# Where the maxima of a chunk are split and turned in a fused attention and GLU kernel: VectorE alone, or VectorE, GpSimd and VectorE in three successive periods

## The chip, the cores and the metric

The kernel runs on one core of a Trainium2 chip. The metric is the time of one execution on the device in microseconds (us), lower is better. The kernel before takes 1719.04 us (median of three runs, 1718.17 to 1721.21).

## What is computed

The input `x` is 2048 tokens by 512 features, all fp32. Half A is a full softmax attention with 32 heads of 16 features. Half B is a GLU with 1792 hidden features. A gate per token mixes the two.

```python
g = sigmoid((x * gate_w).sum(-1, keepdims=True))
qkv = (x @ wqkv).reshape(B, S, 3, H, Dh).transpose(2, 0, 3, 1, 4)
scores = einsum("bhqd,bhkd->bhqk", q, k) * Dh ** -0.5
a = (einsum("bhqk,bhkd->bhqd", softmax(scores), v)).transpose(0, 2, 1, 3).reshape(B, S, D) @ wo
b = einsum("bsf,fd->bsd", sigmoid(x @ w_gate) * (x @ w_up), w_down)
return g * a + (1 - g) * b
```

## The kernel before

**The two passes of the attention.** The softmax needs the largest score of each query before the exponentials are taken. The kernel computes the scores twice. In the first pass (`sm_step`, L271) a matmul (L284) makes a bank of 128 queries by 512 keys in PSUM, and VectorE reduces it to one maximum per query (L286, into the tile `stat`). In the second pass (`st_part`, L561) a matmul (L570) makes the scores the other way round, 128 keys by 512 queries, and ScalarE takes the exponential (L572). The maxima enter the second pass as two more rows of the query operand `QS`: the matmul there has 64 rows, of which 48 hold the split of q, two hold the maximum (its rounded value and the rest that the rounding left), and `KS` holds -1 in the rows that meet them. So the score leaves the matmul with its maximum taken off.

**Chunks.** The heads go in pairs p = 0 to 15, with b = 0 or 1 for the two heads of a pair; head b lies in the partitions 64b and up. The queries go in four blocks i of 512. A chunk is one (p, i, b): 16 banks are reduced for it, into a `stat` tile of 128 x 16. There are 128 chunks. When the last bank of a chunk is reduced, the chunk is put into the list `full`, and `turn_max` (L294) closes it: VectorE reduces `stat` to 128 x 4 (L298, tile `mx`), rounds it to fp32r (L300, tile `msq`), subtracts the rounded from the exact value (L301, `msq`), and transposes 32 x 32 blocks, so that what lay along the partitions lies along a row (L305, tile `mt`). The function that it returns sends the rows with four small DMAs on SyncE's queue (SP) to `QS` (L311). `mx` and `msq` have one buffer each, `mt` has two.

**Periods.** The middle of the kernel is a loop of 256 periods (L774); the first 248 have the same build. A period k issues, in an order written out word by word (`STEADY`, L759), eight matmuls of the first pass (`m0`, `m1`: head 0 and head 1), eight of the second (`t0`, `t1`) and 12 half matmuls of dense work (`d0`, `d1`: first the projections of q and k, then the GLU's first layer), each in its own half of the rows of the PE array. After them come the end of the period (chunks are closed, GpSimd's jobs are issued) and `values(k)` (L692): 32 matmuls of the exponentials with V (L702), whose start marks a period in the profile. Both passes and `values` share seven PSUM banks (`sm`, `st`) in a fixed order, so a matmul there waits until VectorE or ScalarE has emptied its bank; dense work has the bank `dn`.

One chunk closes at the end of each odd period: of head 1 where k mod 4 is 1, of head 0 where it is 3. The first pass runs ahead of the second: the rows of a chunk of head 0 that closes in period k are read by the first `t0` matmul of period k + 5, those of head 1 by a `t1` in the middle of period k + 6.

**Order on the engines.** TensorE, ScalarE, VectorE and GpSimd execute in the order of the code. SP's order comes from the scheduler, and a DMA that waits there holds all that stand behind it. GpSimd's jobs (splits of weights and of x, sums of values, sums of the GLU's parts) are kept in the list `later`, and `work(n)` issues n of them: one at the word `work` in the middle of a period, three or four at its end. In the first 48 periods (the projections) each projection takes two periods; GpSimd then rounds its result (L239) and subtracts (L236), both parts go to DRAM (L238), and the mixed x for the GLU is made, stored (L331) and loaded again (L351) there. Sends of a closed chunk are put at the front of `later`, so that each takes a job's place.

Ahead of the loop, in the rest of V's projection (L577 to L596), the first four chunks and half of a fifth are made; there a closed chunk is turned and sent at once (L588).

Of the kernel before, what the change touches and what calls it, by code (L numbers as in the profile page):

```python
# [12 lines left out]
F32 = mybir.dt.float32  # L13
F32R = mybir.dt.float32r
AF = mybir.ActivationFunctionType
ALU = mybir.AluOpType
# [8 lines left out]
S, D, H, DH, F = 2048, 512, 32, 16, 1792  # L25
P = 128
# [23 lines left out]
def gated_mix(ctx, tc, x, xc, xmix, wqk, wv, wo, w_gu, w_down, gate_w, out):  # L50
    nc = tc.nc
    pe, act, dve, pool, sp = nc.tensor, nc.scalar, nc.vector, nc.gpsimd, nc.sync

    ctx.enter_context(tc.manual_schedule(engines=ORDERED))
    keep = ctx.enter_context(tc.tile_pool(name="keep", bufs=1))
# [133 lines left out]
    def work(n):  # L189
        while later and n:  # L190
            later.pop(0)()
            n -= 1
# [3 lines left out]
    QS, KS = zip(*[(big(f"qs{b}", F32R), big(f"ks{b}", F32R)) for b in range(2)])  # L196
# [45 lines left out]
    def load_pair(p, cols=slice(0, S)):  # L242
        for b in (1, 0):
            for t, src in enumerate((q_d, k_d)):
                rows = slice((2 * p + b) * DH, (2 * p + b + 1) * DH)
                for i, a in enumerate(FORM[t]):
                    r = 64 * b + i * DH
                    yield sp.dma_start((QS, KS)[t][p % 2][r:r + DH, cols].bitcast(F32), src[a, rows, cols])
# [42 lines left out]

    full = []

    def turn_max():  # L294
        part = full.pop(0)
        p, i, b = part
        m, hl = square()
        dve.tensor_reduce(m, stat.pop(part), axis=AX.X, op=ALU.max)  # L298
        two = hl[:, :8].rearrange("p (t c) -> p t c", c=2)
        dve.tensor_copy(two[:, :, 0], m)  # L300
        dve.tensor_tensor(two[:, :, 1], m, two[:, :, 0].bitcast(F32), ALU.subtract)  # L301
        f = hl.bitcast(F32)
        blocks = bass.AP(f.tensor, f.offset, [f.ap[0], (2, 4), (1, 32)])
        mt = keep.tile([P, 4, 32], F32, name=f"mt{p}_{i}_{b}", tag="mt", bufs=2)
        dve.transpose(mt, blocks)  # L305

        def send():
            r = 64 * b + 3 * DH
            rows = QS[p % 2][r:r + 2, i * 512:(i + 1) * 512].bitcast(F32).rearrange("a (t g j) -> a g t j", g=4, j=32)
            for g in range(4):  # L310
                sp.dma_start(rows[:, g], mt[32 * g:32 * g + 2])  # L311
        return send

    SIDES = (slice(0, 64), slice(64, 128))
    def mixing(pair):
# [196 lines left out]
    def first_max():  # L512
        if first:
            j, i = first.pop(0)
            if j < FIRST:
                sm_step(j)(0, i)
                sm_step(j)(1, i)
            else:
                sm_step(j)(1, i)
                sm_step(j + 1)(1, i)  # L520
# [40 lines left out]
    def st_part(k, b):  # L561

        p, r = divmod(k, 16)
        c, kt = divmod(4 * r, 16)
        qs, ks = QS[p % 2], KS[p % 2]
        r = 64 * b
        pt = ptile[k, b] = mid(f"p{k}_{b}")
        for a in range(4):
            o = bank()
            pe.matmul(o, ks[r:r + KR, (kt + a) * P:(kt + a + 1) * P], qs[r:r + KR, c * 512:(c + 1) * 512],  # L570
                      start=True, stop=True)
            act.activation(pt[:, a, :], o, AF.Exp, scale=DH ** -0.5)  # L572
            yield

    ahead = st_part(0, 1)
    bank = bankm
    for t in range(2, NS, 2):  # L577
        two = [Sum(bankv(), tokens(t + a)) for a in range(2)]
        for g in (LOW, UP):
            first_max()  # L580
            for m in range(3 * KT):
                two[0].half(g)
                two[1].half(1 - g)
                if m == 5 or m == 8 and (g == LOW or t == 2):
                    first_max()
                if t == NS - 2 and (g, m) in ((LOW, 8), (UP, 2), (UP, 5), (UP, 8)):
                    next(ahead)
                while full:  # L588
                    turn_max()()
            if g == LOW:  # L590
                turn(*two)
            if t >= 12:
                work(1)
        if t < NS - 2:
            for a in range(2):
                put_v(t + a, two[a].o, act)  # L596


    seven = [maxb[0], maxb[1], banks[2], maxb[2], banks[1], maxb[3], banks[0]]
    bank7 = turns(seven)  # L600
    chunks = [(c, f) for c in range(NC) for f in range(0, NF, 2)]
# [76 lines left out]
    def logit_load(t):  # L678
        tok[t] = keep.tile([P, 2, D], F32, name=f"xn{t}", tag="ev", bufs=2)
        sp.dma_start(tok[t], x[t * P:(t + 2) * P, :].rearrange("(t p) d -> p t d", p=P))  # L680
# [52 lines left out]
    def dense(g):  # L733
        while True:
            if run:
                run.half(g)
            yield

    count_given = [0]

    def place():
        b = given[-REUSE[count_given[0] % len(REUSE)]]
        count_given[0] += 1
        given.append(b)
        return b

    def emit(order, **parts):

        for word in order.split():
            if word == "turn":  # L750
                if run:
                    turn(run)
            elif word == "work":
                work(1)
            else:
                if next(parts[word], place) is place:
                    place()
# [12 lines left out]
    for a, engine in enumerate((act, dve)):  # L770
        put_v(NS - 2 + a, two[a].o, engine)
    bank = bankm = place
    backlog = []
    for k in range(NPER):  # L774
        n = 2 * k
        if n + FIRST == NSTEP:
            bank = bank7
        if 320 <= n < 448 and n % 16 == 0:
            logit_load((n - 320) // 8)
        if n % 32 == 0 and n // 32 + 1 < NPAIR:  # L780
            pair = load_pair(n // 32 + 1)
        if n % 32 <= 10:
            list(islice(pair, 2))
        if k >= NPER - TAIL:
            group["t0"], group["t1"] = st_part(k, 0), st_part(k + 1, 1) if k + 1 < NPER else iter(())
        elif k % 2 == 0:
            group["t0"] = chain(st_part(k, 0), st_part(k + 1, 0))
        else:
            group["t1"] = chain(st_part(k, 1), st_part(k + 1, 1))
        emit(STEADY[k % 2] if k < NPER - TAIL else LAST[k - NPER], **group)  # L790
        turned = []
        while full:
            turned.append(turn_max())
        if run is None:
            pass
        elif run.done():
            run = next(fill, None)
        else:
            turn(run)
        backlog.append(len(later))  # L800
        work(3 if isinstance(run, Sum) and k % 2 else 4)
        later[:0] = turned
        if 320 <= n < 448:
            t = (n - 320) // 16 * 2
            if n % 16 == 2:
                logit_terms(t, 0)
                logit_terms(t, 1)
            elif n % 16 in (8, 10):
                logit_sum(t, (n % 16 - 8) // 2)
        if EARLY <= k < EARLY + 4:  # L810
            early_exp(*divmod(k - EARLY, 2))
        if k == NPER - 1:
# [78 lines left out]
    for n, (c, f) in enumerate(chunks):  # L891
# [4 lines left out]
        hl = ready[n]  # L896
# [68 lines left out]
```

## Time and profile before

| | |
|---|---|
| median of three runs | 1719.04 us (1718.17 to 1721.21) |
| the profiled execution | 1718.9 us, of which the profile's span is 1717.1 us |
| TensorE, VectorE, ScalarE, GpSimd busy | 1702.4, 1498.5, 1338.0, 974.4 us |
| the first pass's reductions on VectorE (L286) | 2048 of 0.68 us, 1325.4 us in all |
| closing of 128 chunks on VectorE (L298, L300, L301, L305) | 125.9 us in all |
| loop of periods | from 90 to 1514 us of the span |
| mean granted TensorE clock | 0.997 of full speed |

Busy times overlap: the sum over the engines says nothing. A matmul's 0.38 to 0.40 us overlaps with its neighbours', so TensorE's busy share doesn't show whether it runs at its peak; the distance between the starts of `values` in two successive periods does. In the rows below, a number in front is the start in us from the beginning of the span, the next is the duration.

### The profile page before, as it was taken

How to read it: one execution, taken by the hardware profiler on the slowest of the kernel's cores; microseconds unless marked ns; L12 is line 12 of the kernel's file. 1: busy time of each engine (PE TensorE's matmuls, PEld its weight loads, DVE VectorE, ACT ScalarE, POOL GpSimd, SP SyncE). 2: the span in 40 equal slices, each digit the busy share in tenths (PEclk: the TensorE clock that was granted, in tenths of full speed). 3: DMA queues.
4: the chain of work that ended last, by engine and by line, in shares of the span. 5: the costliest groups of instructions: out<-in, count | busy, mean ns of one | idle time of the engine just before them, and what ended most of it. 6: DMA issues, size and time to landing. Idle time of an engine off the chain costs nothing.

```text
span 1717.1 us, 43465 instructions
## 1 busy us (share of the span) xinstructions
PE 1702.4 (99%) x16552; PEld 1129.9 (66%) x16552; DVE 1498.5 (87%) x2706; ACT 1338.0 (78%) x2668; POOL 974.4 (57%) x936
## 2 busy tenths in 40 slices
PE   9999999999999999999999999999999999999999
PEld 7866666666666666666666666666666666578887
DVE  6999999999999999999999999999999999566543
ACT  4188787888888888888888889999888888863321
POOL 1045654347787777766665677677676665252110
PEclk9999999999999999999999999999999999999999
DMA  9524575363544454442347232524242423176752
GB/s 256 113 78 167 164 249 155 114 168 119 137 124 132 134 137 122 128 117 69 100 152 213 85 100 92 120 76 123 64 122 75 104 81 110 42 264 223 238 188 70
DMA packets 125008, 228.54 MB, mean 133 GB/s; under 512 B 19008, under 2 KB 35648, under 8 KB 121792
## 3 DMA queue, kind: packets, MB, share of 16 engines
q1 hardware_dynamic: 124512, 225.24, 45.0%
q8 instruction: 131, 2.15, 0.5%
q14 instruction: 77, 0.63, 0.1%
q10 hardware_dynamic: 288, 0.52, 0.1%
HBM read 149.42 MB, written 75.76 MB: 131 GB/s over the span
## 4 chain that ended last, share of the span: by engine, by line
PE 92%; DVE 6%; DMA 1%; ACT 0%; POOL 0%; issue 0%; SPq 0%; POOLq 0%; ACTq 0%
PE dn L170 26%; PE sm L702 20%; PE sm L284 8%; PE st L284 7%; PE sm L901 7%; PE st L702 6%; PE dn L150 4%; DVE stat L286 4%; PE st L137 4%; PE sm L570 3%; PE st L570 2%; PE dn L901 2%; PE st L150 2%; DVE msq L301 1%; DVE mt L305 0%; PE st L84 0%
## 5 line engine op out<-in xcount | busy, mean ns | idle before, releaser
L286 DVE TENSOR_REDUCE stat<-sm 128x1 f32<-128x512 f32 x1124 | 723.2, 677 | 44.2 <-PE st L570 18.7
L572 ACT ACTIVATE p<-sm 128x512 f32<-128x512 f32 x1217 | 688.4, 631 | 11.3 <-PE sm L570 5.9
L286 DVE TENSOR_REDUCE stat<-st 128x1 f32<-128x512 f32 x924 | 602.2, 676 | 33.6 <-PE sm L570 16.6
L572 ACT ACTIVATE p<-st 128x512 f32<-128x512 f32 x831 | 501.5, 636 | 7.4 <-PE dn L150 3.1
L170 PE MATMUL dn<-xm,mh 64*128 64x512 f32 x1568 | 490.9, 392 | 0.0
L570 PE MATMUL sm<-qs,ks 64*128 64x512 f32 x1217 | 456.2, 411 | 3.8 <-DVE stat L286 3.5
L284 PE MATMUL sm<-ks,qs 48*128 48x512 f32 x1124 | 422.7, 424 | 0.3 <-ACT p L572 0.3
L284 PE MATMUL st<-ks,qs 48*128 48x512 f32 x924 | 369.6, 430 | 0.0
L702 PE MATMUL sm<-p,v 128*17 128x256 f32 x6080 | 366.8, 382 | 0.1
L570 PE MATMUL st<-qs,ks 64*128 64x512 f32 x831 | 331.8, 415 | 5.4 <-DVE stat L286 5.4
L720 POOL TENSOR_TENSOR sum<-sum,part 128x256 f32<-128x256 f32 x192 | 141.3, 736 | 320.0 <-ACT part L707 282.6
L170 PEld LDWEIGHTS dn<-xm,mh 64*128 64x128 f32 x1568 | 290.2, 185 | 42.1
L170 PE MATMUL dn<-xm,ml 64*128 64x512 f32 x784 | 308.8, 394 | 0.0
L702 PEld LDWEIGHTS sm<-p,v 128*17 128x17 f32 x6080 | 160.3, 97 | 166.5 <-ACT p L572 53.7
L284 PEld LDWEIGHTS sm<-ks,qs 48*128 48x128 f32 x1124 | 198.9, 185 | 87.8 <-DVE stat L286 52.7
L570 PEld LDWEIGHTS sm<-qs,ks 64*128 64x128 f32 x1217 | 218.2, 186 | 33.3 <-DVE stat L286 14.6
L284 PEld LDWEIGHTS st<-ks,qs 48*128 48x128 f32 x924 | 165.5, 185 | 84.5 <-DVE stat L286 54.3
L403 POOL TENSOR_TENSOR m<-m,m 128x512 f32<-128x512 f32 x140 | 178.1, 1287 | 4.8 <-ACT m L505 4.8
L570 PEld LDWEIGHTS st<-qs,ks 64*128 64x128 f32 x831 | 152.4, 185 | 26.8 <-DVE stat L286 14.0
L170 PEld LDWEIGHTS dn<-xm,ml 64*128 64x128 f32 x784 | 144.6, 184 | 17.7
L123 POOL TENSOR_TENSOR ml<-r,mh 128x512 fp32r<-128x512 f32 x112 | 143.9, 1285 | 7.7
L505 ACT ACTIVATE m<-dn 128x512 f32<-128x512 f32 x196 | 134.0, 684 | 0.0
(225 smaller groups left out, 2201.0 us busy)
## 6 DMA issues: line engine op xcount, KB each, us to landing
r<-in_w_gu_dram SPq DMA_DIRECT2D x112, 256.0 KB
gul<-gu_d SPq DMA_DIRECT2D x56, 512.0 KB
gu_d<-m SPq DMA_DIRECT2D x84, 256.0 KB
xm_d<-xm SPq DMA_DIRECT2D x32, 512.0 KB
xm<-xm_d SPq DMA_DIRECT2D x32, 512.0 KB
xm<-in_xmix_dram SPq DMA_DIRECT2D x24, 512.0 KB
qs<-q_d SPq DMA_DIRECT2D x90, 128.0 KB
ks<-k_d SPq DMA_DIRECT2D x90, 128.0 KB
```

Source lines behind the costliest of these rows:

```text
L123: pool.tensor_tensor(l, src, h.bitcast(F32), ALU.subtract)
L150: mm = pe.matmul(self.o, a[rows], b[rows], start=(self.n == 0), stop=(self.n == 2 * len(self.ops) - 1))
L170: pe.matmul(self.o, a, b, start=(self.n == 0), stop=(self.n == len(self.ops) - 1))
L284: pe.matmul(t, qs[r:r + KM, qt * P:(qt + 1) * P], ks[r:r + KM, g * 512:(g + 1) * 512], start=True, stop=True)
L286: dve.tensor_reduce(stat[part][:, qt % 4, g:g + 1], t, axis=AX.X, op=ALU.max)
L403: pool.tensor_tensor(o, x, y, op)
L505: leave = lambda e, o: act.activation(e, o, AF.Copy)
L570: pe.matmul(o, ks[r:r + KR, (kt + a) * P:(kt + a + 1) * P], qs[r:r + KR, c * 512:(c + 1) * 512], start=True, stop=True)
L572: act.activation(pt[:, a, :], o, AF.Exp, scale=DH ** -0.5)
L702: pe.matmul(o[r:r + VW, :], v[:, 4 * k % 16 + a, h * VW:(h + 1) * VW], pts[b][:, a, 256 * i:256 * i + 256], start=(a == 0), stop=(a == 3))
L720: pool.tensor_tensor(s, s, e, ALU.add)
L901: pe.matmul(down[t], a, b, start=(f == 0 and m == 0), stop=(f == NF - 2 and m == 5))
```

## The change

`turn_max` is divided in three. `close_max` does the reduction to `mx` on VectorE, where all was done before, and gives back two functions. `halves` does the rounding and the subtraction on GpSimd. `turned` does the transposition on VectorE, and gives back the four sends. In the loop, `halves` is put into a new list `urgent`, which is issued at the word `work` of the next period, ahead of the job that `work` issues there and without taking its place. `turned` is called at the end of the second period after the closing, ahead of the closing of the next chunk. The sends go into `urgent` too, and are issued at `work` in the third period. Ahead of the loop, `halves` follows the closing at once, and `turned` and the sends come four steps of the matmul loop later.

```diff
-    def turn_max():
+    def close_max():
         part = full.pop(0)
         p, i, b = part
         m, hl = square()
         dve.tensor_reduce(m, stat.pop(part), axis=AX.X, op=ALU.max)
         two = hl[:, :8].rearrange("p (t c) -> p t c", c=2)
-        dve.tensor_copy(two[:, :, 0], m)
-        dve.tensor_tensor(two[:, :, 1], m, two[:, :, 0].bitcast(F32), ALU.subtract)
...
+        def halves():
+            split(two[:, :, 0], two[:, :, 1], m, pool, pool)
+
+        def turned():
+            f = hl.bitcast(F32)
+            blocks = bass.AP(f.tensor, f.offset, [f.ap[0], (2, 4), (1, 32)])
+            mt = keep.tile([P, 4, 32], F32, name=f"mt{p}_{i}_{b}", tag="mt", bufs=2)
+            dve.transpose(mt, blocks)
...
+        return halves, turned
@@ ahead of the loop @@
-                while full:
-                    turn_max()()
+                if closed:
+                    closed[0][0] -= 1
+                    if closed[0][0] == 0:
+                        closed.pop()[1]()()
+                elif full:
+                    halves, turned = close_max()
+                    halves()
+                    closed.append([4, turned])
@@ emit @@
             elif word == "work":
+                while urgent:
+                    urgent.pop(0)()
                 work(1)
@@ the end of a period @@
-        turned = []
+        jobs = [turned() for turned in stages.pop(0)]
+        stages.append([])
         while full:
-            turned.append(turn_max())
+            halves, turned = close_max()
+            jobs.append(halves)
+            stages[1].append(turned)
...
-        later[:0] = turned
+        urgent.extend(jobs)
```

On VectorE, at the end of period 5, where chunk (0, 3, 1) closes (the numbers of a name `stat_3_1` or `mt_3_1` are i and b, the last is a buffer number, and L298 is the reduction to `mx`), stood before:

```order
L286 TENSOR_REDUCE stat_3_0_1271<-st_65 128x1
L298 TENSOR_REDUCE mx_111<-stat_3_1_1107 128x4
L300 CAST msq_112<-mx_111 128x4
L301 TENSOR_TENSOR msq_112<-mx_111,msq_112 128x4
L305 STREAM_TRANSPOSE mt_3_1_1391<-msq_112 128x128
```

and now:

```order
L286 TENSOR_REDUCE stat_3_0_1263<-st_65 128x1
L308 STREAM_TRANSPOSE mt_2_0_1383<-msq_112 128x128
L298 TENSOR_REDUCE mx_111<-stat_3_1_1103 128x4
L286 TENSOR_REDUCE stat_0_1_1414<-st_67 128x1
```

The two small operations have gone, and the transposition is that of the chunk that closed two periods earlier, (0, 2, 0).

On GpSimd, around the word `work` of period 10 (L330 and L346 were L326 and L342, parts of the mixing of x; L733 is the addition of a period's values to their sum, L720 before), stands now:

```order
L236 TENSOR_TENSOR qk_0_0_0_1698<-qk_0_0_0_1698,qh_0_1700 128x512
L330 TENSOR_TENSOR xm_0_3_1629<-xm_0_3_1629 64x512
L100 CAST msq_112<-mx_111 128x4
L101 TENSOR_TENSOR msq_112<-mx_111,msq_112 128x4
L733 TENSOR_TENSOR sum_2_1647<-sum_2_1647,part_1726 128x256
L346 CAST xm_0_3_1629<-xm_0_3_1629 128x512
```

The rows L100 and L101 are the two small operations; before, the addition to `sum_2` followed on the row of `xm_0_3` at once. They stand ahead of the addition in every second period.

On SP, at the end of the second pair, where chunk (1, 3, 0) of head 0 is sent (it closes in period 23 and is read from period 28 on; `xm` is the mixed x, L321 its load from the input, L331 its store, L351 its load from the store, L238 the store of q or k), stood before:

```order
L238 DMA k_d<-qk_0_1_1_2816 128x512
L351 DMA xm_0_3137<-xm_d 128x2x512
L722 DMA pv_d<-sum_1_2605 128x256
L311 DMA qs_104<-mt_3_0_2814 2x4x32 x4
L351 DMA xm_1_3614<-xm_d 128x2x512 x2
L331 DMA xm_d<-xm_2_2_2819 256x1x512
L351 DMA xm_1_3614<-xm_d 128x2x512 x2
L321 DMA xm_3_0_3060<-in_xmix_dram 128x512
```

and now, where four lines in front are other numbers of the same ones (L355 was L351, L335 was L331, L325 was L321, L314 was L311):

```order
L314 DMA qs_104<-mt_3_1_2808 2x4x32 x4
L735 DMA pv_d<-sum_1_2600 128x256
L355 DMA xm_0_3129<-xm_d 128x2x512
L355 DMA xm_1_3606<-xm_d 128x2x512 x2
L335 DMA xm_d<-xm_2_2_2740 256x1x512
L355 DMA xm_1_3606<-xm_d 128x2x512 x2
L325 DMA xm_3_0_3054<-in_xmix_dram 128x512
L238 DMA q_d<-qh_2_2968 128x512
L238 DMA q_d<-qk_1_0_0_2966 128x512
L314 DMA qs_104<-mt_3_0_2963 2x4x32 x4
```

The sends of (1, 3, 0) have moved behind five loads, a store of the mixed x and two stores of q. Chunk (1, 3, 1) is now sent where (1, 3, 0) was.

More of the change, by code (lines that the diff above doesn't have):

```diff
@@ L299, in turn_max, with send @@
         two = hl[:, :8].rearrange("p (t c) -> p t c", c=2)
[L300 to L312, printed above, removed]
+        def halves():
[5 more added lines that the diff above has]
+            dve.transpose(mt, blocks)
+            def send():
+                r = 64 * b + 3 * DH
+                rows = QS[p % 2][r:r + 2, i * 512:(i + 1) * 512].bitcast(F32).rearrange("a (t g j) -> a g t j", g=4, j=32)
+                for g in range(4):
+                    sp.dma_start(rows[:, g], mt[32 * g:32 * g + 2])
+            return send
+        return halves, turned
     SIDES = (slice(0, 64), slice(64, 128))
@@ L573, in st_part @@
             yield
+    closed = []
     ahead = st_part(0, 1)
@@ L596, in gated_mix @@
                 put_v(t + a, two[a].o, act)
+    for _, turned in closed:
+        turned()()
     seven = [maxb[0], maxb[1], banks[2], maxb[2], banks[1], maxb[3], banks[0]]
@@ L737, in dense @@
             yield
+    urgent = []
     count_given = [0]
@@ L772, in gated_mix @@
     bank = bankm = place
-    backlog = []
+    stages = [[], []]
     for k in range(NPER):
@@ L799, in gated_mix @@
             turn(run)
-        backlog.append(len(later))
         work(3 if isinstance(run, Sum) and k % 2 else 4)
-        later[:0] = turned
+        urgent.extend(jobs)
         if 320 <= n < 448:
```

## The prediction

> **What bounds the kernel now.** I read the page first: which engine is busy, and which makes up the chain that ended last.
>
> ```profile
> PE 1702.4 (99%) x16552; PEld 1129.9 (66%) x16552; DVE 1498.5 (87%) x2706; ACT 1338.0 (78%) x2668; POOL 974.4 (57%) x936
> PE 92%; DVE 6%; DMA 1%; ACT 0%; POOL 0%; issue 0%; SPq 0%; POOLq 0%; ACTq 0%
> ```
>
> TensorE is the bound, but 6% of the chain, some 100 us, runs through VectorE, where the edited instructions are. TensorE's own floor is read from the distance between two starts of `values`. I went through the loop period by period and call the start of `values(k)` S(k). The rows give S(2), S(3) and S(4), then S(79) and S(80):
>
> ```profile
> 101.34 1.92 PE L702 MATMUL sm<-p,v 128*17 128x256 f32 x32
> 106.85 1.92 PE L702 MATMUL sm<-p,v 128*17 128x256 f32 x32
> 113.54 1.92 PE L702 MATMUL sm<-p,v 128*17 128x256 f32 x32
> ...
> 540.31 1.92 PE L702 MATMUL st<-p,v 128*17 128x256 f32 x32
> 546.79 1.92 PE L702 MATMUL sm<-p,v 128*17 128x256 f32 x32
> ```
>
> The distances are 5.51, 6.69 and, later, 6.48. The shortest, 5.51 to 5.52, comes again in most periods, so this is the floor. The long ones, S(k) to S(k + 1) with k mod 4 = 3, hold the closing of a chunk of head 0. What happens there is on VectorE's and GpSimd's timeline, in the period from 106.85 and in that from 540.31:
>
> ```profile
> 108.63 0.17 DVE L298 TENSOR_REDUCE mx<-stat 128x4 f32<-128x16 f32 x1
> ...
> 109.04 1.30 DVE L301 TENSOR_TENSOR msq<-mx,msq 128x4 fp32r<-128x4 f32 x1
> 110.37 0.31 DVE L305 STREAM_TRANSPOSE mt<-msq 128x128 f32<-128x128 f32 x1
> ...
> 542.09 0.17 DVE L298 TENSOR_REDUCE mx<-stat 128x4 f32<-128x16 f32 x1
> 542.29 0.61 DVE L300 CAST msq<-mx 128x4 fp32r<-128x4 f32 x1
> 542.93 0.66 DVE L301 TENSOR_TENSOR msq<-mx,msq 128x4 fp32r<-128x4 f32 x1
> 543.63 0.31 DVE L305 STREAM_TRANSPOSE mt<-msq 128x128 f32<-128x128 f32 x1
> ```
>
> ```profile
> 109.02 1.30 POOL L236 TENSOR_TENSOR qk<-qk,qh 128x512 fp32r<-128x512 f32 x1
> ...
> 541.59 1.28 POOL L403 TENSOR_TENSOR den<-den,m 128x512 f32<-128x512 f32 x1
> 542.84 0.73 POOL L720 TENSOR_TENSOR sum<-sum,part 128x256 f32<-128x256 f32 x1
> ```
>
> VectorE's subtraction of four numbers ends with GpSimd's subtraction of 512: 110.34 and 110.32. At 542 the rounding ends with one GpSimd operation and the subtraction with the next. These two small operations wait for GpSimd's two-input operations. The whole closing took 2.05 us (108.63 to 110.68) and the period was 1.17 over the floor; at 542.09 it took 1.85, and the period 0.96 over. So 0.88 to 0.89 us of a closing is free, and **each microsecond beyond it is paid in full**.
>
> **What the change takes away.** The same operations over all 128 chunks: mean from the groups, median (the middle of three numbers) from the view of a line.
>
> ```profile
> L305 DVE STREAM_TRANSPOSE mt<-msq 128x128 f32<-128x128 f32 x128 | 39.9, 312 | 6.1 <-DVE msq L301 0.8
> L301 DVE TENSOR_TENSOR msq<-mx,msq 128x4 fp32r<-128x4 f32 x128 | 37.0, 289 | 4.4
> L300 DVE CAST msq<-mx 128x4 fp32r<-128x4 f32 x128 | 28.2, 220 | 4.5
> L298 DVE TENSOR_REDUCE mx<-stat 128x4 f32<-128x16 f32 x128 | 20.8, 163 | 2.1
> ...
> 97.67 0.26 DVE L300 CAST msq<-mx 128x4 fp32r<-128x4 f32 x1
> ...
> L301 DVE TENSOR_TENSOR msq<-mx,msq x128: 162/164/1308, 61.8 to 1481.8; 128x4 fp32r<-128x4 f32 x128
> L300 DVE CAST msq<-mx x128: 169/170/819, 61.6 to 1481.6; 128x4 fp32r<-128x4 f32 x128
> ```
>
> Stretching is 128 x (289 - 164) = 16.0 us for L301 and 128 x (220 - 170) = 6.4 for L300, **22.4 us**. About 1 us is within the free part: in the first 48 periods the rounding for head 1 takes 0.26, as at 97.67, and its period stays at the floor: **21.4**. An undisturbed closing of head 0 takes 0.93 (0.17, 0.17, 0.16, 0.31 and the gaps), 0.04 over what is free: 62 of them give **2.5**.
>
> One more loss hangs on a stretched closing, in period 243, where the dense work has run out:
>
> ```profile
> 1454.11 1.92 PE L702 MATMUL sm<-p,v 128*17 128x256 f32 x32
> 1462.41 3.61 PE L702 MATMUL sm<-p,v 128*17 128x256 f32 x32
> 1469.62 1.92 PE L702 MATMUL sm<-p,v 128*17 128x256 f32 x32
> ...
> 1459.00:1466.00 7.00, 6.87 (x42) 3.44 (x42) 4.44 (x8) 2.69 (x5) 3.41 (x4) 0.51 0.27 90
> PEld st L570 <- DVE stat L286: 1.7, 1, 1.7
> ```
>
> TensorE's weight load waited 1.7 us for VectorE, and then the granted clock (third number from the end) was 0.51 for 7 us. The two periods took 15.51, 4.47 over twice 5.52. The stretch in them is 1.7 and already counted; the slow clock's part is **2.8**. In all 21.4 + 2.5 + 2.8 = **26.7 us**. Adding up the excess of every odd period over the floor gives the same within 1 us.
>
> What is late next? After the change VectorE does a transposition (0.31) and a reduction (0.17) there, some 0.5 us with a gap, 0.4 under what is free. So TensorE's floor, 5.52, is next. Periods with k mod 4 = 1 do the same matmuls and reach it with closings of 0.92.
>
> **What it adds on GpSimd.** 256 operations on 4 columns. Nothing of the kind is in the trace. Bounds are a memset of one column, 98 ns, and an addition of 256 columns:
>
> ```profile
> L720 POOL TENSOR_TENSOR sum<-sum,part 128x256 f32<-128x256 f32 x192 | 141.3, 736 | 320.0 <-ACT part L707 282.6
> L403 POOL TENSOR_TENSOR m<-m,m 128x512 f32<-128x512 f32 x140 | 178.1, 1287 | 4.8 <-ACT m L505 4.8
> L954 POOL MEMSET const-float32-1.0<- 128x1 f32 x1 | 0.1, 98 | 0.0
> ...
> 367.12 0.73 POOL L720 TENSOR_TENSOR sum<-sum,part 128x256 f32<-128x256 f32 x1
> ```
>
> From 256 to 512 columns the time goes up by 551 ns, so 4 columns would take 736 - 542 = 194 ns; I take 0.2 each, 0.5 a chunk with gaps, 1.5 at the upper bound. GpSimd sat idle 282.6 us ahead of these very additions, waiting for ScalarE, and that hides it. What waits behind is VectorE's transposition, and with it every reduction and TensorE. The split stands ahead of the addition of its period. The latest addition in the trace started at 367.12, 5.3 us after its S(47), 361.79 by the same view; the transposition comes some 12.5 us after that S, so even operations of 0.74 are in time: I take 0, and keep 2 us for the range. Ahead of the loop VectorE does wait for GpSimd four times, about 0.6 us each, in place of 0.4 of its own; TensorE has other work there: 0, within 1 us either way.
>
> **What it moves: the sends.** A transposition now starts where the closing did, 1.78 after an S (108.63 less 106.85), so it ends about S(k + 2) + 2.1. Head 0 needs the rows when `values` of period k + 4 is through, at S(k + 4) + 1.92, 10.9 us later. Four issues take 2.7 us (below), and a DMA on this queue lands within 1.7 us of its issue: the load of `den` (L671) waits for the store before it.
>
> ```profile
> 1484.39 0.33 SPq L722 DMA_DIRECT2D pv_d<-sum  x1
> ...
> 1486.10 0.51 SPq L671 DMA_DIRECT2D den<-pv_d  x1
> ```
>
> That leaves over 6 us for what SP does ahead. In SP's new order I looked for the places where more stands ahead, with each neighbour's time of before. Everywhere 3 us or more stay, but for one: chunk (1, 3, 0), whose sends now follow the two stores of q (L238) after the crowd of loads.
>
> ```profile
> 244.84 0.34 SPq L321 DMA_DIRECT2D xm<-in_xmix_dram  x1
> ...
> 246.22 2.76 SPq L311 DMA_DIRECT2D qs<-mt  x4
> ...
> SPq L321 <- DMA xm_d<-xm: 4.9, 1, 4.9
> 235.00:245.00 10.00, 10.00 (x112) 6.62 (x104) 9.41 (x19) 8.24 (x18) 6.43 (x7) 1.00 0.96 300
> ...
> 245.37 1.92 PE L702 MATMUL sm<-p,v 128*17 128x256 f32 x32
> ```
>
> SP's load at 244.84 waited 4.9 us for a store of the mixed x, while the DMA engines were 96% busy. The sends at 246.22 were another chunk's; now (1, 3, 0) is issued there, until 248.98, and lands at some 250.4. TensorE wants the rows at S(27) + 1.92 = 247.29. TensorE and this burst both move forward by what was won before, so the distance stays: **a stall of 3.1 us**, between 0 (if the burst clears 3 us sooner) and 6 (if the small DMAs land late). An idle of this length can bring the slow clock, as at 1459: 2.8 us more by that row, 0 at the other end. I take it, since TensorE would be idle for longer than it was there: **5.9** given back.
>
> The Trainium skill, "TensorE: Matmul & The Clock Gate", section "What's actually happening", says that the clock falls to half after at least one idle window of about 3.4 us, and that the windows run freely. By it a stall of 3.1 us need not bring the slow clock, and the sum would be 2.8 less; the row at 1459 has the fall after a shorter wait, so I stay with the row.
>
> **The sum.** 1718.9 - 26.7 + 5.9 = **1698.1 us**, against the profiled execution, whose 1718.9 is 1.8 above its span and 0.1 below the median of the runs, 1719.04. I predict 1698.
>
> **The rivals.** *Stall, full clock*: 1718.9 - 26.7 + 3.1 = 1695.3. *No stall*: the sends land in time, 1692.2; for it speaks that the burst's timing is one execution's, against it the order of SP, which is fixed. *The collision only moves*: VectorE's transposition or reduction of `mx` now meets GpSimd's operations instead, and half of the gain is lost: 1698 + 13 = 1711. Against it: L305's mean of 312 is its undisturbed 0.31, and L298's mean is 163, in all 128 closings, beside a GpSimd that is 57% busy. The Trainium skill, "SBUF — State Buffer", section "Who interferes with whom", draws the line there too: it names two SBUF inputs, and a cast in its two-port mode, as what contends with GpSimd, and says that a reduction never does on trn2; by it this rival gets nothing. *Slower*: the rows of every head-0 chunk miss TensorE. The price is 62 times the lateness, so beyond 26.7 / 62 = 0.43 us of mean lateness the kernel is slower; 1 us gives 1718.9 - 26.7 + 62 = 1754. It decides from about 8 us between the end of a transposition's issues and the landing; the row of 1484.39 has 1.7.
>
> **How the numbers follow.** A measurement tells about 0.2% (3.4 us) from no change. Chances: the forecast with stall and slow clock 0.45, stall at full clock 0.15, no stall 0.27, collision moved 0.07, slower 0.04, no gain at all 0.02. The range takes in the first three and the bounds of the unknown costs (stall up to 6, GpSimd 2, start 1): 1690 to 1705. Faster 0.94, the same 0.02, slower 0.04.
>
> **What would show it.** In the profile after: no group on VectorE of 289 or 220 ns, and 256 small ones on GpSimd near 0.2 us; periods with k mod 4 = 3 at 5.52; the clock at 1.00 between 1430 and 1445. Right or wrong at the stall: the period after S(27) is some 3 us long, with TensorE waiting for the sends. It is wrong as a whole if VectorE's transposition waits for GpSimd (a wait of L308 for L101), or if TensorE waits for the sends at many chunks.

## The result and the profile after

| | before | after |
|---|---|---|
| median of the timed runs | 1720.12 us (4 runs, 1718.17 to 1724.67) | 1696.37 us (4 runs, 1695.47 to 1697.75) |
| ratio after to before | | 0.9859, 95% interval 0.9837 to 0.9881 |
| the profiled execution | 1718.9 us, span 1717.1 | 1697.24 us, span 1695.5 |
| start of the loop, S(0), and of the last `values` | 90.30 and 1512.26 us | 90.66 and 1490.91 us |

The kernel is faster by 23.8 us between the medians and by 21.7 between the two profiled executions; 1698 was predicted. The last `values` starts 21.35 us sooner, though the loop starts 0.36 later.

The page of the changed kernel, its busy times and its chain of waits by engine:

```profile
PE 1686.6 (99%) x16552; PEld 1137.2 (67%) x16552; DVE 1430.5 (84%) x2450; ACT 1335.7 (79%) x2668; POOL 1018.2 (60%) x1192
PE 98%; DMA 1%; ACT 1%; DVE 1%; issue 0%; SPq 0%; POOL 0%; ACTq 0%; POOLq 0%
```

VectorE's 6% of the chain have become 1%. The four operations of a closing, from the groups by line (the last two columns are the busy time with the mean of one, and the engine's idle time just before with what ended it):

```profile
L308 DVE STREAM_TRANSPOSE mt<-msq 128x128 f32<-128x128 f32 x128 | 38.5, 301 | 1.9 <-POOL msq L101 1.9
L298 DVE TENSOR_REDUCE mx<-stat 128x4 f32<-128x16 f32 x128 | 16.3, 128 | 0.0
L101 POOL TENSOR_TENSOR msq<-mx,msq 128x4 fp32r<-128x4 f32 x128 | 26.1, 204 | 10.4
L100 POOL CAST msq<-mx 128x4 fp32r<-128x4 f32 x128 | 24.2, 189 | 219.8 <-DVE mx L298 219.6
```

None of a closing's operations on VectorE is stretched any more. It waits 1.9 us in all for GpSimd, while GpSimd waits 219.6 us for the maxima: its jobs are early, and it has the time. The same place as in the prediction, the period from S(3) (107.20) and what follows it, on TensorE, VectorE and GpSimd:

```profile
107.20 1.92 PE L715 MATMUL sm<-p,v 128*17 128x256 f32 x32
112.72 1.92 PE L715 MATMUL sm<-p,v 128*17 128x256 f32 x32
```

```profile
109.09 0.13 DVE L298 TENSOR_REDUCE mx<-stat 128x4 f32<-128x16 f32 x1
...
119.90 0.30 DVE L308 STREAM_TRANSPOSE mt<-msq 128x128 f32<-128x128 f32 x1
```

```profile
112.12 0.19 POOL L100 CAST msq<-mx 128x4 fp32r<-128x4 f32 x1
112.39 0.20 POOL L101 TENSOR_TENSOR msq<-mx,msq 128x4 fp32r<-128x4 f32 x1
```

The period takes 5.52 where it took 6.69. One chunk goes through it all in 11 us: reduced at 109.09, split by 112.59, turned at 119.90. Read period by period, the distances over 5.515 add up to 28.1 us before (periods 0 to 244) and to 6.4 after. Of the 6.4, one period has 4.95:

```profile
239.61 0.34 SPq L325 DMA_DIRECT2D xm<-in_xmix_dram  x1
...
241.00 2.77 SPq L314 DMA_DIRECT2D qs<-mt  x4
```

```profile
239.78 1.92 PE L715 MATMUL sm<-p,v 128*17 128x256 f32 x32
245.25 0.73 PE L574 MATMUL st<-qs,ks 64*128 64x512 f32 x1 [3.13 <-DMA qs<-mt]
250.24 1.92 PE L715 MATMUL sm<-p,v 128*17 128x256 f32 x32
...
245.00:250.00 5.00, 4.75 (x27) 4.34 (x27) 2.34 (x4) 3.10 (x6) 0.02 (x1) 0.66 0.61 206
```

This is the stall at chunk (1, 3, 0): its sends are issued at 241.00, behind a load that waited 6.0 us for a store of the mixed x and could not start until 239.61. TensorE waits 3.13 us for them, and the granted clock is 0.66 in the 5 us that follow (0.50 from 245.28 to 248.70). S(27) to S(28) takes 10.46.

At the other end, S(243), S(244) and S(245), with the window from 1435 to 1445:

```profile
1437.20 1.92 PE L715 MATMUL sm<-p,v 128*17 128x256 f32 x32
1442.71 1.92 PE L715 MATMUL sm<-p,v 128*17 128x256 f32 x32
1448.23 1.92 PE L715 MATMUL sm<-p,v 128*17 128x256 f32 x32
...
1435.00:1445.00 10.00, 10.00 (x101) 6.14 (x98) 9.08 (x17) 8.82 (x19) 7.40 (x10) 1.00 0.34 120
```

5.51 and 5.52 in place of 8.30 and 7.21, at full clock.

### The profile page after: what moved, and what is told of

Read it like the earlier page. It is cut to its first block, busy times and chain, and to the rows that moved or that the text cites. A ratio compares the mean times of both kernels' runs of the same rounds, so it can differ in the third digit from the quotient of the medians.

```text
span 1695.5 us, 43423 instructions
## 1 busy us (share of the span) xinstructions
PE 1686.6 (99%) x16552; PEld 1137.2 (67%) x16552; DVE 1430.5 (84%) x2450; ACT 1335.7 (79%) x2668; POOL 1018.2 (60%) x1192
## 3 DMA queue, kind: packets, MB, share of 16 engines
q8 instruction: 131, 2.15, 0.6%
## 4 chain that ended last, share of the span: by engine, by line
PE 98%; DMA 1%; ACT 1%; DVE 1%; issue 0%; SPq 0%; POOL 0%; ACTq 0%; POOLq 0%
PE dn L170 25%; PE sm L715 21%; PE sm L284 8%; PE st L284 8%; PE st L715 7%; PE sm L919 7%; PE dn L150 6%; PE st L137 4%; PE sm L574 4%; PE st L574 3%; PE dn L919 2%; PE st L150 2%; DMA xm<-xm_d 1%; ACT p L576 0%; DVE stat L286 0%; PE st L84 0%
## 5 line engine op out<-in xcount | busy, mean ns | idle before, releaser
L574 PE MATMUL sm<-qs,ks 64*128 64x512 f32 x1217 | 445.7, 404 | 0.4 <-ACT p L576 0.2
L574 PE MATMUL st<-qs,ks 64*128 64x512 f32 x831 | 326.0, 410 | 3.1 <-DMA qs<-mt 3.1
L733 POOL TENSOR_TENSOR sum<-sum,part 128x256 f32<-128x256 f32 x192 | 141.9, 739 | 86.5 <-ACT part L720 59.3
L100 POOL CAST msq<-mx 128x4 fp32r<-128x4 f32 x128 | 24.2, 189 | 219.8 <-DVE mx L298 219.6
```

Of the source, the lines that this page charges most:

```text
L733: pool.tensor_tensor(s, s, e, ALU.add)
```

## The experiments

Open after the result were: whether the stall hangs on the place of the sends; whether moving to another engine or to another time brings the gain; whether the rule "0.88 us free, then one to one" holds; how much room the sends have; and what brings the slow clock. Times are medians; a ratio is to the runs of the kernel before on the same chip.

### The stall: the transposition one period sooner

```diff
-    stages = [[], []]
+    stages = [[]]
...
-            stages[1].append(turned)
+            stages[-1].append(turned)
```

> The changed kernel with the transposition one period earlier (GpSimd's halves and VectorE's transposition in the same period after the closing), so that chunk (1, 3, 0)'s sends stand on SP ahead of the load of xm that waited for a store until 239.6 us. Theory (the period after S(27) is long because those sends land late, 3.13 us of waiting and 1.8 us of slow clock): that period goes back to 5.52 and the time falls by 4.95, to about 1691.5. Rival (the DMA crowd of that place would hold the sends up wherever they stand, or TensorE waits there for something else): the period stays near 10, the time near 1696.4. Second rival (GpSimd isn't done in time, and VectorE waits for it): the longest delay from a closing to the end of the halves in the changed kernel is some 4.9 us and the transposition would come 5.5 after the closing, so I expect VectorE to wait for GpSimd for under 3 us in all; if it waits for more than 0.9 us in many periods, the time is above 1700.

Measured: 1693.01 us (4 runs, 1691.04 to 1693.28), ratio 0.9848 (0.9831 to 0.9864). The issues on SP, S(27) and S(28), and VectorE's transposition by line:

```profile
230.11 3.23 SPq L314 DMA_DIRECT2D qs<-mt  x4
237.23 0.33 SPq L325 DMA_DIRECT2D xm<-in_xmix_dram  x1
```

```profile
239.08 1.92 PE L715 MATMUL sm<-p,v 128*17 128x256 f32 x32
244.59 1.92 PE L715 MATMUL sm<-p,v 128*17 128x256 f32 x32
...
L308 DVE STREAM_TRANSPOSE mt<-msq 128x128 f32<-128x128 f32 x128 | 38.4, 300 | 2.4 <-POOL msq L101 2.4
```

The sends go out at 230.11, ahead of the load that is held until 237.23, and the period is 5.51. The profiled execution, 1691.04, is where 1691.5 was expected, but it is the fastest of the four: the median is 1.5 above that, and 3.4 below the changed kernel's 1696.37 on another chip. No period but three of 0.2 is over the floor. VectorE waits 2.4 us in all for GpSimd: the change turns a chunk two periods after its closing, and one is enough.

### The split on VectorE, only moved in time

```diff
-            split(two[:, :, 0], two[:, :, 1], m, pool, pool)
+            split(two[:, :, 0], two[:, :, 1], m, dve, dve)
```

> The changed kernel with both halves on VectorE in place of GpSimd: the deferral over three periods alone. Theory (a period has about 0.88 us of free VectorE time, wherever in it the work falls): the split moves from the periods with closings into those without, 0.16 + 0.17 us undisturbed; stretched by GpSimd's operations as before (means 0.29 and 0.22, up to 1.3) it goes over 0.88 only in the few worst cases, so the time is 1697 to 1701, at most 5 above the changed kernel. Rival (the stretching is paid wherever it falls, and only the other engine brings the gain): about 16 to 21 us of the gain are lost, 1712 to 1718.

Measured: 1754.49 us (4 runs, 1749.35 to 1758.45), ratio 1.0203 (1.0177 to 1.0229). Both expectations missed it: slower than the kernel before. The two operations by line, and one of the places, on VectorE, GpSimd and TensorE:

```profile
L100 DVE CAST msq<-mx 128x4 fp32r<-128x4 f32 x128 | 78.6, 614 | 0.2
L101 DVE TENSOR_TENSOR msq<-mx,msq 128x4 fp32r<-128x4 f32 x128 | 65.8, 514 | 4.4
```

```profile
463.24 0.98 DVE L100 CAST msq<-mx 128x4 fp32r<-128x4 f32 x1
464.25 1.20 DVE L101 TENSOR_TENSOR msq<-mx,msq 128x4 fp32r<-128x4 f32 x1
...
461.66 2.53 POOL L407 TENSOR_TENSOR m<-m,m 128x512 f32<-128x512 f32 x2
464.14 1.29 POOL L380 TENSOR_TENSOR r<-r,r 128x512 f32<-128x512 f32 x1
...
463.97 1.92 PE L715 MATMUL sm<-p,v 128*17 128x256 f32 x32
470.72 1.92 PE L715 MATMUL st<-p,v 128*17 128x256 f32 x32
```

The rounding ends with GpSimd's second addition (464.22 and 464.19), the subtraction with the one after it (465.45 and 465.43). The split took 2.21 us from 463.24, and the next period 6.75, 1.24 over. So 0.97 is free here; the same comes out at the other long splits (1.64 gives 0.67 and 1.33 gives 0.35, so 0.97 and 0.98). The even periods, which had no closing, are 54.5 us over in all. The rule held; what failed is the size that I put in, the mean stretching of the kernel before. Laying VectorE's timeline over GpSimd's shows what differs: before, 76 of the 128 roundings and 98 of the 128 subtractions began while GpSimd was idle, and here 35 and 45 (gaps of GpSimd under 0.15 us are counted as busy).

### The split on VectorE, moved to the end of the next period

```diff
+        while waiting:
+            waiting.pop(0)()
         jobs = [turned() for turned in stages.pop(0)]
...
-            jobs.append(halves)
+            waiting.append(halves)
```

(with the two halves on VectorE as above)

> The halves on VectorE as in the run before that came out at 1754, but at the end of the period after the closing, not 4.78 us into it, in the middle. There the split lasted 0.35 us alone and 2.2 us when it met GpSimd twice, and what it took above 0.98 was paid in the next period. Theory (the place decides how often GpSimd is met: right there GpSimd has just been handed its next operations): at the end of a period the stretching is that of the kernel before, which did the split at such a place (0.29 and 0.22 on average), over 0.98 in few periods, so 1697 to 1708. Rival (VectorE's small operations meet GpSimd as often anywhere outside a closing, or a period without a closing has less room): 1735 or more.

Measured: 1738.10 us (2 runs), ratio 1.0111 (1.0081 to 1.014). The rival was right:

```profile
L100 DVE CAST msq<-mx 128x4 fp32r<-128x4 f32 x128 | 70.9, 554 | 0.2
L101 DVE TENSOR_TENSOR msq<-mx,msq 128x4 fp32r<-128x4 f32 x128 | 49.3, 385 | 4.4
```

42 roundings and 67 subtractions found GpSimd idle; the even periods are 38 us over in all. So the kernel before had its split at a place where GpSimd often stood still (it waited 282.6 us for ScalarE ahead of its additions), and the places tried here are worse ones. At both places tried, moving the split in time alone loses; better places on VectorE may exist, and were not looked for.

### The split on GpSimd at once, nothing moved in time

```diff
 (before)
-        dve.tensor_copy(two[:, :, 0], m)
-        dve.tensor_tensor(two[:, :, 1], m, two[:, :, 0].bitcast(F32), ALU.subtract)
+        split(two[:, :, 0], two[:, :, 1], m, pool, pool)
```

> The kernel before with both halves on GpSimd at once and nothing deferred: VectorE's transposition stands right behind and waits for GpSimd. Theory (whatever holds VectorE above 0.88 us in a closing is paid): a closing takes at least 0.13 + 0.46 + 0.2 + 0.3 = 1.1 us with GpSimd free (0.46 is the commonest delay from the closing to the subtraction's start in the changed kernel), some 0.5 more with GpSimd busy or waiting in its own queue; 128 closings with 0.2 to 0.9 over give 25 to 110 us on the floor of 1692, so 1717 to 1800, slower than the changed kernel in any case. Rival (GpSimd's speed and freedom from collisions alone bring the gain, the stages nothing): at or below 1700.

Measured: 1707.73 us (4 runs, 1705.31 to 1713.3), ratio 0.9929 (0.9914 to 0.9944); neither expectation had that. A closing of head 0 on VectorE and GpSimd, the two `values` around it, and GpSimd's waiting by line:

```profile
561.70 0.17 DVE L298 TENSOR_REDUCE mx<-stat 128x4 f32<-128x16 f32 x1
562.44 0.31 DVE L304 STREAM_TRANSPOSE mt<-msq 128x128 f32<-128x128 f32 x1 [0.57 <-POOL msq L101]
...
561.94 0.19 POOL L100 CAST msq<-mx 128x4 fp32r<-128x4 f32 x1 [2.43 <-DVE mx L298]
562.21 0.20 POOL L101 TENSOR_TENSOR msq<-mx,msq 128x4 fp32r<-128x4 f32 x1
...
559.92 1.92 PE L701 MATMUL st<-p,v 128*17 128x256 f32 x32
565.61 1.92 PE L701 MATMUL sm<-p,v 128*17 128x256 f32 x32
...
L100 POOL CAST msq<-mx 128x4 fp32r<-128x4 f32 x128 | 24.1, 188 | 442.2 <-DVE mx L298 442.2
```

A closing takes 1.05 us (561.70 to 562.75), 0.17 over 0.88, and the period 5.69, 0.17 over. Nearly all periods of head 0 are the same, those of head 1 0.04 over. My 0.5 us for a busy GpSimd was wrong: it stands at the split and waits (442.2 us, 128 times), so it is always free when the maxima come, and meets nothing. 62 times 0.17 and 62 times 0.04 give 13 us over the floor of 1692: 1705. In the profiled execution (1713.3) one more period is 6.6 us over: GpSimd waited 7.38 us for a load of `xm`, and TensorE 3.68 us for a signal that GpSimd's queue gives. So the other engine alone brings some 11 us (1718.77 on this chip less 1707.73), and the move out of VectorE's line the rest.

### No split at all

```diff
 (before)
-        dve.tensor_reduce(m, stat.pop(part), axis=AX.X, op=ALU.max)
         two = hl[:, :8].rearrange("p (t c) -> p t c", c=2)
-        dve.tensor_copy(two[:, :, 0], m)
-        dve.tensor_tensor(two[:, :, 1], m, two[:, :, 0].bitcast(F32), ALU.subtract)
+        dve.tensor_reduce(two[:, :, 0], stat.pop(part), axis=AX.X, op=ALU.max)
```

> The kernel before, with the last reduction writing its maxima straight into the rounded columns: neither the rounding nor the subtraction exists on any engine, the sends stay where they were before, nothing is deferred. The low halves of the maxima stay zero: what is subtracted ahead of the exponential is then the rounded maximum, which softmax cancels. Theory (all of the loss was the part of a closing above 0.88 us, and what is left, a reduction and a transposition of some 0.5 us, fits): all odd periods at 5.52, no long period after S(27), so 1720 - 26.7 = about 1693 less the 1.8 us for the slow clock that I may have put too high, 1692 to 1695; faster than the changed kernel by 2 to 5 us. Rival (the gain needs the move to another period, since the wait for the last reduction and the transposition are what holds VectorE): periods with k mod 4 = 3 stay over 5.6 and the time is above 1700.

Measured: 1691.29 us (4 runs, 1690.35 to 1691.81), ratio 0.9836 (0.9822 to 0.9851). What is left of a closing, at once and in line as before, from the views of two lines (minimum, median, maximum in ns, and the first and last start):

```profile
L299 DVE TENSOR_REDUCE msq<-stat x128: 155/165/171, 61.3 to 1452.7; 128x4 fp32r<-128x16 f32 x128
L303 DVE STREAM_TRANSPOSE mt<-msq x128: 311/311/314, 61.5 to 1452.9; 128x128 f32<-128x128 f32 x128
```

Neither is ever stretched, the rounding in the reduction costs nothing (163 ns on average, as without it), and the periods over the floor add up to 0.7 us, with no stall, since the sends stay where they were. Beside the changed kernel on one chip:

> The changed kernel once more, timed beside the next one on one chip: 1696.4 by its first timing, with the period after S(27) near 10.5 again (a wait of about 3.1 for the sends of chunk (1, 3, 0), then the slow clock for about 1.8).

> The kernel whose last reduction writes straight into the rounded columns (no low halves, no split, nothing deferred), timed beside the changed kernel. Theory (both have every closing below 0.88 us, and the difference is the stall with its slow clock, 4.95, less what differs ahead of the loop): faster than the changed kernel by 4 to 6 us, 1690 to 1692. Rival (the first comparison, across two jobs, was off): within 2 us of each other.

Measured: the changed kernel 1697.19 us (5 runs, 1693.8 to 1698.33; ratio 0.9876, 0.9857 to 0.9894), the one without a split 1692.52 (4 runs, 1691.57 to 1692.9; ratio 0.9846, 0.9827 to 0.9864). It is 4.7 us faster, the ranges apart, as expected, though the time itself is 0.5 above the 1692 that I had put as its upper end: **it beats both kernels**, with fewer instructions and no new order. (It takes off a rounded maximum, which is harmless as the same number is taken off in every score of a query.)

The second trace of the changed kernel also shows what varies:

```profile
243.50 0.47 PE L574 MATMUL st<-qs,ks 64*128 64x512 f32 x1 [2.35 <-DMA qs<-mt]
```

The stall is 2.35 this time, the granted clock stays at 1.00 in the windows from 240 to 255, and S(27) to S(28) is 8.30: 2.8 us given back where the first execution gave back 4.95. My expectation of 10.5 missed this.

### Doses at a closing

```diff
+        scores = stat.pop(part)
+        closings.append(part)
+        for _ in range(DOSE.get(len(closings), 0)):
+            dve.tensor_reduce(load, scores, axis=AX.X, op=ALU.max)
-        dve.tensor_reduce(m, stat.pop(part), axis=AX.X, op=ALU.max)
+        dve.tensor_reduce(m, scores, axis=AX.X, op=ALU.max)
```

> The changed kernel with a dose at 13 of the 128 closings: the last reduction (0.13 us) is done 2, 4, 6, 8, 10 or 12 times more into a tile that nobody reads, at k = 51, 59, 67, 75, 83, 91 (head 0), at k = 101, 109, 117, 125, 133, 141 (head 1), and 12 times at k = 243. The trace is read, not the time. Theory (a closing costs nothing up to 0.88 to 0.89 us with head 0, about 1.0 with head 1, and beyond that one to one; with 0.35 for the transposition and the reduction and 0.12 for each one more): periods with head 0 long by 0, 0, 0.2, 0.4, 0.7, 0.9, with head 1 by 0, 0, 0.1, 0.3, 0.5, 0.8 us, each within 0.15. At 243, where the dense work has run out: 0.9 of waiting, and if the slow clock of the kernel before there came from TensorE's wait, some 2.8 more over periods 243 and 244; if it came from elsewhere, the two periods are 0.9 over in all and the granted clock stays at 1.00. Rival to the rule (a closing is a threshold: VectorE either keeps up or a buffer turns late, with a jump): periods jump by 0.5 or more at once, then stay. In time about 1697 + 3.9, or with the slow clock + 6.7.

Measured (one profiled execution, 1708.41 us). The closing with six more reductions, and S(67) and S(68):

```profile
467.77 0.30 DVE L316 STREAM_TRANSPOSE mt<-msq 128x128 f32<-128x128 f32 x1
468.00 1.15 DVE L305 TENSOR_REDUCE load<-stat 128x4 f32<-128x16 f32 x6
...
469.14 0.68 DVE L286 TENSOR_REDUCE stat<-sm 128x1 f32<-128x512 f32 x1
...
466.11 1.92 PE L723 MATMUL st<-p,v 128*17 128x256 f32 x32
472.10 1.92 PE L723 MATMUL sm<-p,v 128*17 128x256 f32 x32
```

| reductions more | 2 | 4 | 6 | 8 | 10 | 12 |
|---|---|---|---|---|---|---|
| head 0, period over 5.515 by (us) | 0 | 0.06 | 0.48 | 0.88 | 1.29 | 1.71 |
| head 1 | 0 | 0.06 | 0.48 | 0.88 | 1.29 | 1.70 |

From the transposition's start to the next reduction of a bank VectorE is taken for 1.37 us, and the period is 0.48 over: 0.89 free. A reduction costs 0.19 to 0.20 us with its gap, not 0.12, so each step of two, 0.4, comes back as 0.4, and all the doses together cost 10.5 us, not 3.9. The rule holds, with no jump, and head 1 has the same 0.89 by this measure. The 0.88 of head 0 and the 1.0 of head 1 in the kernel before are another measure, from the start of a closing's first operation to the end of its last, and operations of VectorE that follow at once overlap by some 0.08 us. From the end of one bank's reduction to the start of the next, the free part is 0.84 to 0.85 for both heads before, and 0.81 to 0.82 for both here. So how much is free doesn't depend on the head.

At k = 243 the period is 7.22, 1.70 over, and the next 5.52. TensorE's wait there, and two windows around it (the first number behind the length is TensorE's busy time):

```profile
1450.99 0.49 PE L582 MATMUL st<-qs,ks 64*128 64x512 f32 x1 [1.22 <-DVE stat L286]
...
1447.07:1450.48 3.41, 2.70 (x24) 1.47 (x16) 3.03 (x17) 2.78 (x6) 2.98 (x3) 1.00 0.51 176
1450.48:1453.89 3.41, 2.90 (x22) 1.45 (x26) 3.41 (x7) 2.38 (x6) 3.25 (x7) 1.00 0.25 94
```

Nearly the same wait as in the kernel before (1.25 us), and no slow clock. So was the slow clock of the kernel before an accident of one execution?

> The kernel before once more, for a second trace. Question: the slow clock of 2.8 us in its periods 243 and 244. It stood behind a wait of TensorE of 1.25 us; in the run with doses a wait of 1.22 at the same place left the clock at 1.00, and in the other traces one wait of 1.51 brought it and one of 1.51 and one of 1.89 did not. Theory (after a wait of 1.2 to 1.9 us it is chance): the closing at k = 243 is again stretched by 1.0 to 1.7 us and the wait is there, and the clock after it may be 1.00; then periods 243 and 244 are 1.7 over instead of 4.47 and the loop is 2.8 shorter. Rival (something fixed at that place of this kernel brings it): 0.5 again for some 7 us, 4.4 over.

Measured (one profiled execution, 1720.95 us): the wait is 1.25 us and ends at 1459.54; the window that holds it, and the next:

```profile
1456.69:1460.10 3.41, 2.15 (x10) 1.22 (x7) 3.34 (x6) 2.34 (x6) 3.41 (x5) 1.00 0.67 242
1460.10:1466.92 6.82, 6.82 (x42) 3.47 (x42) 3.75 (x6) 3.05 (x6) 2.74 (x3) 0.50 0.19 58
```

The two periods took 15.55 us, 4.5 over twice 5.52, as in the first trace. The rival is right as far as two traces go: at that place of the kernel before it comes again.

The record of the granted clock shows what the dosed kernel had otherwise. In every trace the clock changes only at the borders of stretches of 3.41 us, which follow one another without a gap through the whole execution, and whose place shifts between executions; the windows above are such stretches (the last is two). In both traces of the kernel before, the wait lies almost whole in one stretch, in which TensorE is busy for 2.23 us (from 1455.65) and 2.15 us. In the dosed kernel the border at 1450.48 cuts the wait, and 2.70 and 2.90 are left. Over all traces, from S(0) to S(244), the clock fell ten times, always behind a stretch with TensorE busy for 2.23 us or less; behind all other stretches it stayed, and only two of these had so little, 1.84 and 1.88. So where a wait lies among the borders counts beside its length. It is not busy time alone that counts: after S(244), where the dense work has run out, the clock fell also behind stretches with 0.5 us idle or less. What exactly is counted stays open.

### The sends one period later

```diff
-    stages = [[], []]
+    stages = [[], [], []]
...
-            stages[1].append(turned)
+            stages[-1].append(turned)
```

> The changed kernel with the transposition, and so the sends, one more period later (5.52 us). It is the slower rival's mechanism, dosed. Theory (the rows must have landed at S(k + 4) + 1.92, and land some 1.4 us after the last issue: 243.77 to 245.12 in the changed kernel): there the last issue ended 8.3 us ahead of that point in most chunks of head 0 from k = 47 on, so 2.8 are left and 1.4 of these spare; no loss at those. Late are the places where less than 6.9 were left: with k below 47 (6.3 to 6.4, about 0.5 late each, if SP still holds the sends up for 2 us there), and k = 51, 75, 79, 91, 107, 147 (2.7 to 5.5 left: 1.4 to 4.2 late), 10 to 20 us in all, besides the stall at (1, 3, 0), which stays or grows by up to 5.5. So 1700 to 1725, unevenly spread. Rival (the slack is smaller than I read, since the rows are needed earlier or land later): every period with k mod 4 = 3 is long, 62 times 1 us or more, above 1755.

Measured: 1714.46 us (8 runs, 1713.56 to 1716.4), ratio 0.9974 (0.996 to 0.9987). What TensorE waited for, in us in all, times, and the longest:

```profile
PE st L574 <- DMA qs<-mt: 11.4, 4, 7.6
PE sm L574 <- DMA qs<-mt: 4.0, 3, 1.9
```

Seven waits, not 62: 15.4 us. S(27) to S(28) is 10.1 over; the rest is about 14, nearly all in the periods 19, 59, 63, 71, 75, 87 and 147. A period is late by the chunk that closed four periods earlier, so these are the chunks of k = 15, 55, 59, 67, 71, 83 and 143. The bulk of the chunks is still in time with 5.5 us less, as the 8.3 us that I read off said. The total is in the range, but none of the six places that I named came: what stands ahead of the sends on SP moved with the edit. The last issue for the chunk of k = 55 came 0.1 us ahead of the point of need, where 8.3 less 5.5 leaves 2.8, and that for k = 51 came 2.7 ahead, where it would have been late.

## Why the prediction was right, point by point

- **What bounds.** TensorE's floor of 5.51 to 5.52 is reached in all but five periods of the changed kernel, the long ones with k mod 4 = 3 were the closings, and the free part of 0.88 to 0.89 with one-to-one beyond it is shown by the doses, by the split in line (1.05 gives 0.17) and by the moved split (with 0.97 in a period without a closing).
- **The gain, 26.7.** Over the floor were 28.1 us before; what is left of that after, beside the stall, is 1.4. The difference, 26.7, is the predicted sum. That the two small operations were the cause is shown by the kernel without a split, which has no other edit and the same floor. That their length beyond 0.17 us came from GpSimd is shown by their ends: all 48 that took over 0.25 us end within 0.04 us of the end of one of GpSimd's operations, and of the other 208 only seven do.
- **The 2.8 for the slow clock** in it was there in both traces of the kernel before and gone after. That TensorE's wait brings it is shown in part: a wait nearly as long in the dosed kernel brought none, and there it was cut by a border of the clock's stretches.
- **GpSimd.** 0.2 us each was taken; 0.189 and 0.204 were measured. The cost of nothing held: VectorE waits 1.9 us in all.
- **The start** cost 0.36, within the 1 us.
- **Given back, 5.9.** The mechanism and the chunk were right, and sends that go out sooner end it. The stall's size was right too (3.1 predicted, 3.13 measured), but that it was met so closely is luck: with the same edit it was 2.35 in the second trace. The term that was **mis-sized** is "2.8 us more" for the slow clock: it was 1.8 (4.95 less 3.13), since I carried over the size from the place at 1459, where the clock stayed at half for two stretches, from 1459.06 to 1465.89; here it did for one, from 245.28 to 248.70. In the second trace, with the stall of 2.35, the clock stayed full, so two of my three cases, with and without the slow clock, are two executions of one kernel.
- **The sum.** 26.7 less 4.95 less 0.36 is 21.4, which is the loop's 21.35; 1698.1 was 0.9 above the profiled execution for the 1.0 of the clock.
- **The rivals.** *The collision only moves* got nothing: VectorE's transposition and reduction are at 301 and 128 ns on average, never above 313 and 160. What the Trainium skill says in "SBUF — State Buffer", section "Who interferes with whom", agrees, and the rows show it for the cast and the two-input operation alike. *Slower* did not come, and a period later still it comes at a few places only.
- **What I did not see**: the place of the split in the kernel before was a good one. My view of the collisions as a fixed mean for each operation gave the right sum, since the change takes both operations off VectorE, but was wrong by 30 to 57 us as soon as they were put elsewhere on VectorE (1738 for 1697 to 1708, 1754 for 1697 to 1701).

## What to carry to other kernels

Read from the floor of a period how much of a second engine's work is free, count the rest one to one, and ask of a stretched operation whether it has to be there at all before it is moved: here the output type of the reduction did what two operations, a second engine and three stages did, without late sends. A stretching by a neighbour belongs to the place, not to the operation, so its mean can't be taken along when the operation moves on the same engine. Where an edit moves DMAs, read the queue's new order against what holds it up: one group of sends behind a blocked load gave back almost a fifth of the gain.

## What the runs showed of the hardware

- A rounding or a two-input operation of 4 columns on VectorE that meets GpSimd's operations ends with one of them: 0.16 us alone, up to 1.31 before, and 2.21 where the moved rounding met two of GpSimd's back to back (659.17 to 661.69; the rounding from 659.51 to 661.72). Of the 48 such operations over 0.25 us in the kernel before, all end within 0.04 us of the end of one of GpSimd's.
- A reduction of 16 columns to 4 and the transposition on VectorE are not touched: at most 172 and 317 ns in all traces. A reduction that writes the rounded type takes as long as the other (163 ns on average).
- The last reduction of a chunk takes 128 ns on average behind a transposition, and 163 behind the reduction of the bank whose result it reads.
- The granted clock changed only at the borders of stretches of 3.41 us that follow one another from the start to the end of an execution, and was at half for one, two or three of them (3.41, 6.83 and 10.24 us).
- After waits of TensorE of 2.6 us and more the granted clock fell every time (seven in all traces); the period lost 1.8 us beyond the wait in four of them and 2.5 to 2.9 in the three others. After waits of 1.2 to 2.4 us it fell in some cases (1.25 at 1459, twice, and 1.51) and not in others (1.22, 1.51, 1.89 and 2.35); the 1.22 was cut by a border, the two of 1.25 lay almost whole in one stretch.
